# A long convolution whose weight rows hold two lags 1024 apart, and a ring of its own for VectorE's linear terms

## The chip, the cores and the metric

The kernel runs on one core of one Trainium2 chip. The metric is the device time of one execution in microseconds (us). The time before is the median of three executions, 815.14 us (814.76 to 815.46). The profile was taken in one further execution, with a time of its own, 807.64 us.

## The reference

Two independent blocks share one output of 2048 x 1024 in bf16; each fills 512 of its columns.

```python
# A: attention, S = 2048, D = 512, 32 heads of 16
qkv = x @ wqkv                              # (2048, 1536)
p = softmax(q @ k.T * 16 ** -0.5)           # per head, 2048 x 2048
a = concat_heads(p @ v) @ wo
# B: gated long convolution, per channel c of 512
k_shift[t] = sum_j k[t - j] * shift_k[c, j]          # 4 taps
kv = k_shift * v
y[t] = sum_{l <= t} ssm_k[c, l] * kv[t - l] + ssm_D[c] * kv[t]   # through an FFT of 4096
b = q * y
out = concat(a, b)
```

## The kernel before, in words

**Attention.** Work is cut into 2048 blocks of 128 keys x 512 queries of one head, 64 blocks for each of 32 groups (`NQB * NG`). A counter `T` counts chunks. For each chunk TensorE (the score matmuls of `qk_mm`, line 796) writes two or three blocks of scores into banks of PSUM, and ScalarE takes the exponential of all of them in one instruction (`emit_exp`, line 821) and writes bf16 into a ring of `R_PT` slots, `PT`. Two sets of three banks alternate, so that ScalarE works on one while TensorE fills the other. Two chunks later `pv_step` and `emit_pv` (line 970) multiply `PT` with V and add into bank `PVB`; at the end of a group VectorE transposes the sums (line 1041), divides and transposes back.

**Exponentials on VectorE.** In some chunks one more block (`dve_block`, `exp_on_dve`) goes to bank `BGB` or to the third bank, and VectorE computes its exponential. Line 884 moves the scores out as bits (`lin`). Then two such blocks, a pair of 128 x 1024, take five operations: `mant` (892), `power` (896), `line` (899), `square` (902) and `cube` (905). A block done so enters the product with V as three terms, `lin`, `low` and `top`, so as three matmuls instead of one. The three terms of a pair lie in the ring `PTD` of `R_PTD` = 3 pairs; the mantissa lies in one buffer, `FR`, so `mant` of a pair waits for `square` of the pair before (`h_last`).

**Convolution.** 64 steps (`qd`) take eight channels each. The reversed convolution kernel lies in a scratch in DRAM; each row of the ring `WR` (`R_W` = 12 rows of 2048, four rows for a step) is one DMA of 512 KB from it: 64 copies, each shifted by one element more, of the kernels of two channels, on alternate partitions. `conv_lags` (line 1187) multiplies `WR` with `KV`. `KV` holds kv of two channels side by side with zeros between, so half of each weight tile is zero. A step has 32 lags (`NLAG`), and a lag is four matmuls of 128 columns, one for each strip of 32 columns of the array. After a burst of two steps `conv_out` (line 1207) copies the sums to `YB`; after four steps `conv_turn` (line 1219) transposes them, VectorE multiplies with q (line 1226), and they go out through `QN`. `kv` itself comes from units `("kv", c, i)`: line 512 applies the four taps with matmuls of 128 columns, line 561 multiplies with v in two halves, and `spread_kv` lays it out in `KV` with four DMAs for each quarter of the channels.

**What sets the order.** A planner in Python writes out the order of every engine beforehand. It keeps an assumed time of its own for each engine and each DMA, and it puts projections, convolution, VectorE blocks and fillers where they fit in front of the next exponential: `emit_qk`, `late_block`, `pv_step`, `emit_bg` (units and convolution, with due times from `jobs`, `conv_due` and `PLAN`), `release` (loads of `WR`) and `warm_up` (fillers without use, line 1382) for each `T`. Loads of `WR` are issued by SyncE (SP), the loads of q and the results by GpSimd (POOL). On the chip each engine runs its list in that order and waits on semaphores.

Of the kernel before, what the change touches and what calls it, by code (L numbers as in the profile page):

```python
# [13 lines left out]
S = 2048  # L14
# [13 lines left out]
NLAG = S // 64  # L28
# [4 lines left out]
R_W = 12  # L33
R_PT = 16
# [8 lines left out]
LEAD = 2  # L43
YIELD = -4
FIRST = 6
BURST = 2
OVER_C = 0.0
HURRY = 2
LOW = 4.5
# [20 lines left out]
R_PTD = 3  # L70
# [12 lines left out]
PLAN = 588  # L83
# [4 lines left out]
GAP = 5  # L88
# [7 lines left out]
DMA_KB = 394  # L96
X_KB = 200
# [157 lines left out]
def bass_concat_heads__mha_block__ssm_conv_h3__prompt_kernel(  # L255
# [24 lines left out]
    def sb(name, shape, dt=BF16):  # L280
# [9 lines left out]
    WR = sb("WR", [128, R_W, S])  # L290
# [3 lines left out]
    QN = QNF[:, 0:NB * 256].rearrange("p (t d) -> p t d", t=NB)  # L294
# [13 lines left out]
    PTD = sb("PTD", [128, R_PTD, 3, 2, QB])  # L308
    FR = sb("FR", [128, 2 * QB])
# [7 lines left out]
           for x in (WR[:, R_W - 2, :], WR[:, R_W - 1, :], OUTA[:, :, :].rearrange("p r d -> p (r d)"), VS2[:, :])]  # L317
# [9 lines left out]
    KVF = KV[:, :, :, :, :].rearrange("p o r u g -> p (o r u g)")  # L327
    STG = [KVF[:, 32 * S // 16 * ((c + 1) % 4):32 * S // 16 * ((c + 1) % 4 + 1)].rearrange(
        "p (h o u k g) -> p h o u k g", h=2, o=16, u=NB, k=2) for c in range(4)]
    XN = FR[:, :].rearrange("p (j f) -> p j f", j=2)  # L330
# [66 lines left out]
    d_wr = [DmaSem(sem(f"d_wr{i}")) for i in range(3)]  # L397
# [25 lines left out]
    for c in range(4):  # L423
        src = bass.AP(tensor=v2.tensor, offset=v2[128 * (NB - 1), 128 * c].offset, ap=[[D, 128], [-128 * D, NB], [1, 128]])
        h_vn.append(dma(sp, d_kv[3 + c], VST[c], src, kb=512))
# [18 lines left out]
    h_kv0 = [None, None]  # L444
    h_kv0[0] = pool.op(lambda e: e.memset(KV[:, :, :, :, :].rearrange("p o r u g -> p (o r u g)").bitcast(U32), 0), us=(8.8, 8.9))
# [25 lines left out]
    def ready(u):  # L471
# [8 lines left out]
        return KT_OF[u[1]][0] in h_kt and (u[1] < 3 or h_kv0[1] is not None and at(h_kv0[1]) <= pe.t)  # L480

    def pe_unit(u, bank, parts=(0, 1, 2, 3)):
# [19 lines left out]
        elif kind == "kv":  # L502
# [5 lines left out]
            def mm(e, b):  # L508
                ins = None
                for m in range(4):  # L510
                    c0 = LEFT + 128 * (4 * i + 3 - b) - m
                    ins = e.matmul(PS[:, bank, 128 * b:128 * b + 128], lhsT=KTR[kt_i][:, kt_c, c0:c0 + 128], rhs=DG[:, c, m, :],  # L512
                                   start=(m == 0), stop=(m == 3))
                return ins
# [19 lines left out]
    def evac_unit(u, bank, h):  # L534
# [18 lines left out]
        elif kind == "kv":  # L553
            _, c, i = u
            u0 = NB - 4 - 4 * i
            val = VST[c][:, u0:u0 + 4, :].rearrange("p b (h o g) -> p b h o g", h=2, g=4)
            src = PS[:, bank, :].rearrange("p (b h o g) -> p b h o g", b=4, h=2, g=4)
            for ch in range(2):
                dst = STG[c][:, ch, :, u0:u0 + 4, ch, :].rearrange("p o u g -> p u o g")
                hh = (dve.op if ch else urgent)(  # L560
                    lambda e, dst=dst, ch=ch: e.tensor_tensor(dst, src[:, :, ch], val[:, :, ch], ALU.mult),
                    [h, h_vn[c], h_kv0[c // 3]], us=(0.335, 0.46))
# [3 lines left out]
            if sum(kv_n[0:2]) == 8 and c < 2:  # L566
                load_qn(0, [h])
                open_wr(2, hh, True)
# [13 lines left out]
    def spread_kv(c, hh):  # L582
        for half in range(2):
            for ch in range(2):
                src = STG[c][64 * half:64 * half + 64, ch].rearrange("p o u k g -> p o (u k g)")
                dst = KV[ch:128:2, 16 * c:16 * c + 16, 1 - half, :, :].rearrange("p o u g -> p o (u g)")
                h_kvc[c] = dma(sp, d_kvc[c], dst, src, [hh, h_kvc[c - 1] if c else None] if half + ch == 0 else [], kb=256, rate=210)
# [20 lines left out]
    def kz_store(us):  # L608
# [4 lines left out]
        open_wr(R_W - 2, h_kzw[0])  # L613
# [111 lines left out]
    def emit_qk(T):  # L725
# [12 lines left out]
        bl = next_blocks(n + (extra in next_blocks(n)))  # L738
        if extra in bl:
            bl.remove(extra)  # L740
# [30 lines left out]
    def next_blocks(n):  # L771
        bl = []
        for b in [b for b in queue[:LOOK] if blk_group(b) == blk_group(queue[0])] + queue[:n]:
            if len(bl) < n and b not in bl and (blk(b)[2] not in [blk(x)[2] for x in bl] or len(bl) + 1 > 4):
                bl.append(b)
        for b in queue[:n]:
            if len(bl) < n and b not in bl:
                bl.append(b)
        return bl
# [55 lines left out]
    def conv_due():  # L835
        return N_OPEN + state["qd"] * (PLAN - N_OPEN) / (C // 8)

    def conv_wants(T):
        qd = state["qd"]
        return (state["started"] and T >= conv_due() - YIELD and qd < C // 8 and wr_next[0] >= qd + BURST and h_kvc[qd // 16] is not None  # L840
                and at(h_wr[qd + BURST - 1], h_kvc[qd // 16]) + WAIT < pe.t + 1.0 and not (state["turn"] and qd % 4 == 4 - BURST))

# [3 lines left out]
    def dve_block(T, n_act, aside=True):  # L846
        if T < T_DVE or aside and busy() or len(queue) < LAST_BLKS + 3 * TAIL_GAP + 4:
            return None
        if aside and conv_wants(T):
            return None  # L850
# [8 lines left out]
        bl = next_blocks(n_act + 1)  # L859
        x = sub(bl[-1])  # L860
        left = len([b for b in queue if sub(b) == x])
        if left - 3 >= 2.6 * GAP:
            return bl[-1]
# [6 lines left out]
        rows = [blk(b)[2] for b in bl[:-1]]  # L870
        ahead = [b for b in ahead[:4] if b not in bl]
# [646 lines left out]
```

## Time and profile before

| What | Before |
|---|---|
| median of three executions | 815.14 us |
| profiled execution, its own time | 807.64 us |
| its span, first to last instruction | 805.7 us |
| ScalarE (ACT) busy | 784.9 us |
| VectorE (DVE) busy | 715.1 us |
| TensorE (PE) busy, matmul | 745.7 us |
| mean share of the 16 DMA engines, queue of SP | 58.2% |
| mean granted TensorE clock | 0.999 |

In rows of groups, the numbers after the bar are the busy time of the group in us (the time that its instructions cover together), the mean time of one in ns, and the time that the engine sat idle just before them, with what ended it. An instruction can start before the one ahead of it on its engine has ended, so its mean time is longer than the distance from one start to the next.

### The profile page before, as it was taken

What the parts mean: (1) busy time and instruction counts of PE and PEld (TensorE: products, weight loads), DVE (VectorE), ACT (ScalarE), POOL (GpSimd) and SP (SyncE); (2) the same over time, 40 slices, a digit from 0 to 9 for tenths busy, and PEclk for the clock granted to TensorE, in tenths of its full rate; (3) what the DMA queues carried; (4) which work ended last, traced back from release to release, by engine and by line L of the source; (5) the groups of instructions that cost most, each with busy time, mean ns of one, the idle gap of its engine ahead of it and who ended that gap; (6) DMA issues with size and microseconds to landing.
All of it is one profiled execution on the core that took longest, in us unless ns stands there. A gap on an engine that the chain in (4) does not pass through costs nothing.

```text
span 805.7 us, 31982 instructions
## 1 busy us (share of the span) xinstructions
PE 745.7 (93%) x14505; PEld 337.1 (42%) x14505; DVE 715.1 (89%) x1427; ACT 784.9 (97%) x680; POOL 90.4 (11%) x160
## 2 busy tenths in 40 slices
PE   8889998999998989999999989989989899999987
PEld 3333444435444433444433434434443434434444
DVE  5989999999798989898898989889999899889986
ACT  7999999999999999999999999999999999999997
POOL 6200402020100101020010030101003020000000
PEclk9999999999999999999999999999999999999999
DMA  9995277846877671446845657985684663876310
GB/s 244 204 306 175 63 184 227 287 108 215 265 261 240 215 243 59 156 115 235 267 142 206 213 168 254 308 281 193 227 299 138 212 224 129 283 260 216 110 55 28
DMA packets 88101, 161.44 MB, mean 200 GB/s; under 512 B 49216, under 2 KB 53184, under 8 KB 87584
## 3 DMA queue, kind: packets, MB, share of 16 engines
q1 hardware_dynamic: 80976, 150.43, 58.2%
q0 software_dynamic: 5792, 8.66, 3.7%
q8 instruction: 114, 1.87, 0.9%
q10 hardware_dynamic: 1200, 0.33, 0.2%
q14 instruction: 19, 0.16, 0.1%
HBM read 142.87 MB, written 6.42 MB: 185 GB/s over the span
## 4 chain that ended last, share of the span: by engine, by line
ACT 79%; PE 14%; DVE 5%; issue 1%; DMA 1%
ACT PT L821 79%; PE PS L970 5%; PE PS L796 4%; PE PS L1187 1%; DVE PTD L884 1%; DMA QN<-in_B_k_dram 1%; PE PS L512 1%; PE PS L1115 1%; PE PS L630 0%; PE PS L491 0%; DVE PTD L902 0%; DVE DT L1041 0%; DVE PTD L905 0%; DVE FR L892 0%; DVE PTD L896 0%
## 5 line engine op out<-in xcount | busy, mean ns | idle before, releaser
L821 ACT ACTIVATE PT<-PS 128x1024 bf16<-128x1024 f32 (+1 forms) x674 | 781.9, 1362 | 11.5 <-PE PS L796 10.8
L796 PE MATMUL PS<-QT,KTo 32*128 32x512 bf16 (+2 forms) x2248 | 265.6, 364 | 39.8 <-ACT PT L821 17.5
L884 DVE TENSOR_SCALAR PTD<-PS 128x512 uint16<-128x512 f32 x326 | 219.2, 682 | 49.2 <-PE PS L796 47.8
L1187 PE MATMUL PS<-WR,KV 128*26 128x128 bf16 (+9 forms) x8192 | 191.2, 219 | 0.7 <-issue 0.6
L970 PE MATMUL PS<-PT,VA 128*32 128x512 bf16 (+2 forms) x1889 | 184.6, 369 | 5.0 <-DVE DT L1041 2.1
L1187 PEld LDWEIGHTS PS<-WR,KV 128*32 128x32 bf16 (+8 forms) x8192 | 140.6, 94 | 52.9 <-issue 29.8
L796 PEld LDWEIGHTS PS<-QT,KTo 32*128 32x128 bf16 x2248 | 69.6, 91 | 205.0 <-ACT PT L821 150.4
L970 PE MATMUL PS<-PTD,VA 128*32 128x512 bf16 (+1 forms) x1077 | 121.0, 360 | 3.9 <-issue 3.9
L902 DVE TENSOR_TENSOR PTD<-FR,PTD 128x1024 f16<-128x1024 bf16 (+1 forms) x164 | 112.3, 685 | 4.0
L905 DVE TENSOR_TENSOR PTD<-PTD 128x1024 bf16<-128x1024 f16 (+1 forms) x164 | 111.5, 680 | 1.9
L352 POOL DMA_DIRECT2D QT<-QS x120 | 60.4, 511 | 443.7 <-DVE QS L539 443.7
L970 PEld LDWEIGHTS PS<-PT,VA 128*32 128x32 bf16 x1889 | 47.4, 93 | 100.8 <-issue 85.5
L892 DVE TENSOR_SCALAR FR<-PTD 128x1024 uint16<-128x1024 uint16 (+1 forms) x164 | 69.0, 421 | 3.5
L896 DVE TENSOR_SCALAR PTD<-PTD 128x1024 uint16<-128x1024 uint16 (+1 forms) x164 | 68.9, 420 | 0.0
L1382 PE MATMUL PS<-IDN,ZW 128*32 128x512 bf16 (+3 forms) x297 | 67.4, 310 | 1.3 <-issue 1.0
L899 DVE TENSOR_SCALAR PTD<-FR 128x1024 f16<-128x1024 bf16 (+1 forms) x164 | 68.1, 415 | 0.0
L970 PEld LDWEIGHTS PS<-PTD,VA 128*32 128x32 bf16 x1077 | 44.8, 96 | 33.2 <-issue 4.4
L1382 PEld LDWEIGHTS PS<-IDN,ZW 128*32 128x32 bf16 x297 | 23.4, 96 | 23.3 <-issue 12.2
L1041 DVE STREAM_TRANSPOSE DT<-PS 128x512 f32<-128x512 f32 x31 | 22.1, 713 | 5.6 <-PE PS L970 5.3
L352 POOL DMA_DIRECT2D out_dram<-OUTA x15 | 8.6, 575 | 97.2 <-DVE OUTA L1123 93.1
L1115 PE MATMUL PS<-WKV,OTN 128*128 128x512 bf16 (+1 forms) x68 | 19.0, 371 | 0.3 <-DVE OTN L1090 0.3
L523 PE MATMUL PS<-WKV,xT 128*128 128x128 bf16 x256 | 18.3, 220 | 0.4 <-DVE KTo L548 0.3
(75 smaller groups left out, 259.3 us busy)
## 6 DMA issues: line engine op xcount, KB each, us to landing
WR<-kz_scratch SPq DMA_DIRECT2D x256, 512.0 KB, 5.8
KV<-KV SPq DMA_DIRECT2D x16, 256.0 KB, 5.4
kz_scratch<-WR SPq DMA_DIRECT2D x1, 2176.0 KB, 8.8
QN<-in_B_q_dram POOLq DMA_DIRECT2D x2, 1024.0 KB, 7.6
out_dram<-QN POOLq DMA_DIRECT2D x2, 1024.0 KB, 8.3
QT<-QS POOLq DMA_DIRECT2D x120, 16.0 KB, 3.3
out_dram<-OUTA POOLq DMA_DIRECT2D x15, 128.0 KB, 2.0
QN<-in_B_ssm_k_dram SPq DMA_DIRECT2D x1, 1024.0 KB, 8.3
```

What stands on the lines that cost most here:

```text
L352: f(outp, inp).then_inc(dsem.sem, 16)
L796: ins = e.matmul(PS[:, bank, i * w:i * w + w], lhsT=KTo[32 * s:32 * s + 32, OF[n_] % 2, kt * 128:(kt + 1) * 128], rhs=QT[32 * s:32 * s + 3 ...
L821: h_exp[T] = act.op(lambda e: e.activation(PT[:, p0:p0 + n, :].rearrange("p b f -> p (b f)"), PS[:, banks[0]:banks[0] + n, :].rearrange("p ...
L884: st["h"].append(urgent(lambda e: e.tensor_scalar(lin[:, QB * half:QB * half + QB].bitcast(U16), PS[:, bank, :], FIX_ADD, FIX_HI, ALU.add, ...
L892: st["d"] = st["m"] = dve.op(lambda e: e.tensor_scalar(FR[:, w].bitcast(U16), lin[:, w].bitcast(U16), 0x7F, 0x3F80, ALU.bitwise_and, ALU.b ...
L896: dve.op(lambda e: e.tensor_scalar(low[:, w].bitcast(U16), lin[:, w].bitcast(U16), 0xFF80, None, ALU.bitwise_and), [st["h"][-1]], us=us)
L899: st["d"] = dve.op(lambda e: e.tensor_scalar(top[:, w].bitcast(FP16), FR[:, w], T1, T0, ALU.mult, ALU.add), [st["m"]], us=us)
L902: st["d"] = h_last[j] = dve.op(lambda e: e.tensor_tensor(top[:, w].bitcast(FP16), FR[:, w], top[:, w].bitcast(FP16), ALU.mult), [st["d"]], ...
L905: st["d"] = dve.op(lambda e: e.tensor_tensor(top[:, w], top[:, w].bitcast(FP16), lin[:, w], ALU.mult), [st["d"]], us=us)
L970: ins = e.matmul(dst, lhsT=w, rhs=rhs, start=first, stop=last, tile_position=(0, 32 * s))
L1187: ins = e.matmul(PS[32 * g:32 * g + 2 * ((30 - d) // 2 + 1), BGB, c0:c0 + w], lhsT=kv, rhs=WR[:, (4 * qd + g) % R_W, S - 64 * d - 128:S - ...
L1382: pe.op(lambda e, s=s, k=k, rhs=rhs, bank=bank, rows=rows, c0=c0, first=first: e.matmul(PS[32 * s:32 * s + rows, bank, c0:c0 + 128 * k], l ...
```

## The change

- `KV` holds kv of one channel group with no second channel and no zeros between: partitions 0 to 63 hold one half, and partitions 64 to 127 the positions 1024 away. A row of `WR` is 1024 wide: its first 64 partitions start at lag 0, the last 64 at lag 1024. `R_W` is 24 rows of 256 KB, so the ring has its old size.
- A step now takes four channels, so there are 128 (`NQD`). It has eight lags (`NLAG` = 8); a lag is again four matmuls with 128 columns to stream, whose results go to two runs of 64 columns. A burst is four steps. The steps alternate between two quarters of the channels (`kv_of`), so the convolution starts when two quarters of kv are there.
- `spread_kv` is one DMA for a quarter instead of four, and line 561 is one operation of 512 instead of two of 256; the taps are matmuls with weight tiles of 64 columns, twice as many. `YB` is copied 512 at a time, and `conv_turn` uses matmuls with a permuted identity, two instead of one transpose. The clearing of a part of `KV` in mid-run is gone. The loads of q and the stores of b through `QN` are cut in two halves of 64 partitions.
- VectorE's pairs: `lin` has a ring of its own, `PTD` of five pairs; `low` and `top` lie in `RST` of three pairs (`R_RST`); `FR` is gone: the mantissa lies where `low` will be, and the order is now mant, line, square, power, cube. `PT` has 14 slots instead of 16.
- The planner chooses the rows of blocks so that they differ (`next_blocks`, `pick_row`), and some of its numbers change.

```diff
-NLAG = S // 64
+NLAG = S // 256
+NQD = C // 4
-R_W = 12
-R_PT = 16
+R_W = 24
+R_PT = 14
-FIRST = 6
-BURST = 2
+FIRST = 4
+BURST = 4
-LOW = 4.5
+LOW = 3.5
-R_PTD = 3
+R_PTD = 5
+R_RST = 3
-PLAN = 588
+PLAN = 600
-GAP = 5
+GAP = 7
...
-    KV = sb("KV", [128, C // 8, 2, 2 * NB, 4])
+    KV = sb("KV", [128, NQD, 2 * NB, 4])
-    PTD = sb("PTD", [128, R_PTD, 3, 2, QB])
-    FR = sb("FR", [128, 2 * QB])
+    PTD = sb("PTD", [128, R_PTD, 2, QB])
+    RST = sb("RST", [128, R_RST, 2, 2, QB])
...
-                    ins = e.matmul(PS[:, bank, 128 * b:128 * b + 128], lhsT=KTR[kt_i][:, kt_c, c0:c0 + 128], rhs=DG[:, c, m, :],
-                                   start=(m == 0), stop=(m == 3))
+                    for x in range(2):
+                        c0 = LEFT + 64 * (4 * i + 3 - b) + S // 2 * x - m
+                        ins = e.matmul(PS[64 * x:64 * x + 64, bank, 128 * b:128 * b + 128], lhsT=KTR[kt_i][:, kt_c, c0:c0 + 64],
+                                       rhs=DG[:, c, m, :], start=(m == 0), stop=(m == 3), tile_position=(0, 64 * x))
...
+        src = KV[0:64, 32 * c:32 * c + 32, 0:NB, :].rearrange("p q w g -> p q (w g)")
+        dst = KV[64:128, 32 * c:32 * c + 32, NB:2 * NB, :].rearrange("p q w g -> p q (w g)")
+        h_kvc[c] = dma(sp, d_kvc[c], dst, src, [hh, h_kv0, h_kvc[c - 1] if c else None], kb=256, rate=KV_KB)
...
-            row = 128 * (qd // 16) + 4 * (qd % 16) + g
-            src = bass.AP(tensor=kz_ap.tensor, offset=kz_ap[row, 0].offset, ap=[[1, 64], [64 * LKZ, 2], [1, S]])
-            h_wr[qd] = dma(sp, d_wr[qd % 3], WR[:, n % R_W, :], src, [h_kzw[0], dep, h], kb=512, rate=WR_KB, late=2.95)
+            src = bass.AP(tensor=kz_ap.tensor, offset=kz_ap[channel(qd) + g, 0].offset, ap=[[S // 2, 2], [1, 64], [1, S // 2]])
+            h_wr[qd] = dma(sp, d_wr[qd % (R_W // 4)], WR[:, n % R_W, :], src, [h_kzw[0], dep, h], kb=256, rate=WR_KB, late=2.95)
...
             for n in range(n0, n1):
-                d = DIST[n]
-                w = 64 if d < 0 else 128
                 for g in range(4):
-                    kv = KV[:, qd, (1 + d) % 2, (1 + d) // 2 * 2:2 * NB, g]
-                    ins = e.matmul(PS[32 * g:32 * g + 2 * ((30 - d) // 2 + 1), BGB, c0:c0 + w],
-                                   lhsT=kv, rhs=WR[:, (4 * qd + g) % R_W, S - 64 * d - 128:S - 64 * d - 128 + w],
+                    dst = PS[32 * g:32 * g + 32 - 2 * n, BGB, :]
+                    c0 = 256 * (1 - pair) + 64 * (1 - half)
+                    dst = bass.AP(tensor=dst.tensor, offset=PS[32 * g:32 * g + 1, BGB, c0:c0 + 1].offset, ap=[dst.ap[0], [128, 2], [1, 64]])
+                    w0 = S // 2 - 128 * n - 128
+                    ins = e.matmul(dst, lhsT=KV[:, channel(qd) // 4, 2 * n:2 * NB, g], rhs=WR[:, (4 * qd + g) % R_W, w0:w0 + 128],
                                    start=(n == 0), stop=(n == NLAG - 1), tile_position=(0, 32 * g))
...
-                ins = e.transpose(pbf[:, 128 * k:128 * k + 128], YB[:, b % 2, 128 * k:128 * k + 128], IDN[:, :])
+                for part in range(2):
+                    y = YB[:, k // 2, 256 * (k % 2) + 128 * part:256 * (k % 2) + 128 * part + 128]
+                    ins = e.matmul(PS[:, bank, 128 * k + 4 * part:128 * k + 128], lhsT=y, rhs=(own, next_)[part], start=part == 0, stop=part == 1)
...
-        begin = lambda: (n == 2 or st["alone"]) and (j == 0 or j - 1 in h_last)
+        begin = lambda: (n == 2 or st["alone"]) and (j < R_RST or all((j - R_RST, i) in h_ptd for i in range(len(pairs[j - R_RST]["h"]))))
...
-        if aside and conv_wants(T):
+        if aside and conv_wants(T) and (state["go"] or conv_due() < T - PRESS):
```

More of the change, by code (lines that the diff above doesn't have):

```diff
@@ L858, in dve_block, with pick_row @@
             return None
[L859 to L860 removed]
+        def pick_row(of, most):
+            mine = [b for b in of if sub(b) == sub(of[0])][:most]
+            there = [blk(b)[2] for b in on_dve if sub(b) == sub(of[0]) and on_dve[b] not in h_ptd]
+            return min(mine, key=lambda b: there.count(blk(b)[2]))
+        x = sub(queue[min(n_act, len(queue) - 1)])
         left = len([b for b in queue if sub(b) == x])
+        if left - 3 >= 2.6 * GAP and sub(queue[0]) == x:
+            return pick_row(queue, LOOK)
         if left - 3 >= 2.6 * GAP:
[L863 removed]
+            return pick_row(queue[n_act:], 4)
         if x == subs[-1]:
@@ L869, in dve_block @@
             return None
-        rows = [blk(b)[2] for b in bl[:-1]]
-        ahead = [b for b in ahead[:4] if b not in bl]
-        return next((b for b in ahead if blk(b)[2] not in rows), ahead[0] if ahead else None)
+        return pick_row(ahead, 4)
     h_last = {}
@@ L949, in emit_pv @@
             pv_n[(n, s)] = pv_n.get((n, s), 0) + 1
-            terms = [PTD[:, on_dve[b][0] % R_PTD, i, on_dve[b][1], :] for i in range(3)] if b in on_dve else [PT[:, pt_of[b], :]]
+            terms = [PT[:, pt_of[b], :]] if b not in on_dve else [PTD[:, on_dve[b][0] % R_PTD, on_dve[b][1], :]] + [
+                RST[:, on_dve[b][0] % R_RST, i, on_dve[b][1], :] for i in range(2)]
             hl = 2 * s + n % 2
@@ L991, in conv_done @@
     def conv_done():
-        return state["qd"] == C // 8 and not state["turn"] and not part[0]
+        return state["qd"] == NQD and not state["turn"] and not part[0]
     def pv_step(T):
```

159 lines of the change are left out of this document (79 added, 80 removed).

## The prediction

> **What bounds the kernel now.** I read the page first, its parts 1, 4 and 5, then the groups of ScalarE with the shapes kept apart, then who waits for whom.
>
> ```profile
> span 805.7 us, 31982 instructions
> PE 745.7 (93%) x14505; PEld 337.1 (42%) x14505; DVE 715.1 (89%) x1427; ACT 784.9 (97%) x680; POOL 90.4 (11%) x160
> ...
> ACT 79%; PE 14%; DVE 5%; issue 1%; DMA 1%
> ...
> L821 ACT ACTIVATE PT<-PS 128x1024 bf16<-128x1024 f32 (+1 forms) x674 | 781.9, 1362 | 11.5 <-PE PS L796 10.8
> L884 DVE TENSOR_SCALAR PTD<-PS 128x512 uint16<-128x512 f32 x326 | 219.2, 682 | 49.2 <-PE PS L796 47.8
> L1187 PE MATMUL PS<-WR,KV 128*26 128x128 bf16 (+9 forms) x8192 | 191.2, 219 | 0.7 <-issue 0.6
> L970 PE MATMUL PS<-PTD,VA 128*32 128x512 bf16 (+1 forms) x1077 | 121.0, 360 | 3.9 <-issue 3.9
> L1382 PE MATMUL PS<-IDN,ZW 128*32 128x512 bf16 (+3 forms) x297 | 67.4, 310 | 1.3 <-issue 1.0
> ```
>
> ScalarE carries 79% of the chain that ended last. Its exponentials cover 781.9 of 805.7 us, and in the whole run they waited only 11.5 us, nearly all of it for TensorE's scores. So the span is the exponentials (781.9), their waits (11.5) and about 12 us at the two ends. TensorE looks as busy, but 67.4 us of it are fillers (line 1382), and VectorE is idle for 805.7 − 715.1 = 90.6 us, of which 49.2 lie before line 884: it waits for a block to work on.
>
> ```profile
> L821 ACT ACTIVATE PT<-PS 128x1536 bf16<-128x1536 f32 x374 | 524.9, 1558 | 2.8 <-PE PS L796 2.5
> L821 ACT ACTIVATE PT<-PS 128x1024 bf16<-128x1024 f32 x300 | 301.1, 1117 | 8.7 <-PE PS L796 8.3
> ```
>
> ScalarE does 374 x 3 + 300 x 2 = 1722 of the 2048 blocks, VectorE 326. The waits sit on the short exponentials: 8.7 us over 300 (29 ns each) against 2.8 over 374 (7.5 ns).
>
> **ScalarE, which sets the end.** The written order of the changed program has 438 exponentials of three blocks, 191 of two and one of one: 1697 blocks in 630 instructions. VectorE takes 351 blocks, 25 more. I need the distance from one exponential to the next.
>
> ```profile
> 31.16 12.19 ACT L821 ACTIVATE PT<-PS 128x1536 bf16<-128x1536 f32 x9
> 789.36 6.73 ACT L821 ACTIVATE PT<-PS 128x1024 bf16<-128x1024 f32 x7
> 796.35 1.02 ACT L821 ACTIVATE PT<-PS 128x1024 bf16<-128x1024 f32 x1 [0.25 <-PE PS L796]
> 797.83 2.88 ACT L821 ACTIVATE PT<-PS 128x1024 bf16<-128x1024 f32 x3 [0.46 <-PE PS L796]
> ```
>
> In the timeline (start, length, then the merged instructions) nine of three blocks take 12.19 us: (12.19 − 1.56) / 8 = 1.329. For two blocks the rows give (2.88 − 1.117) / 2 = 0.88 and (6.73 − 1.117) / 6 = 0.936; spreading 781.9 − 374 x 1.329 over 300 gives 0.95, small stalls included. I take 0.915, the middle. A single one is about 0.915 − 0.441 = 0.47, with 0.441 the difference of the two means. The sum: 64 x 1.329 − 109 x 0.915 + 0.47 = 85.1 − 99.7 + 0.5 = −14.1 us. With 0.88 it is −10.4, with 0.95 −18.0. Both ends of the run stay as they are.
>
> The waits of 11.5 us: by the new mix, 191 x 29 ns + 438 x 7.5 ns = 8.8, a gain of 2.7. Against it stands a fuller VectorE, below, whose price no row gives. I set the two against each other and keep 11.5; the bounds are 0 and, in the rival, well above.
>
> **TensorE, beside it.**
>
> ```profile
> 399.87 0.63 PE L1187 MATMUL PS<-WR,KV 128*14 128x128 bf16 x32
> ...
> 400.79 0.51 PE L1187 MATMUL PS<-WR,KV 128*6 128x128 bf16 x24
> ...
> L512 PE MATMUL PS<-OTN,QN 128*128 128x128 bf16 x128 | 9.4, 220 | 1.6 <-DMA QN<-in_B_k_dram 1.0 <-DVE KV L561 0.3 <-DVE PTD L884 0.3
> L1219 PE MATMUL PS<-IDN,YB 128*128 128x128 bf16 x64 | 6.4, 222 | 1.4 <-DVE YB L1207 1.4
> ```
>
> Eight convolution matmuls more take 0.63 − 0.51 = 0.12 us, so a lag of four takes 0.06. The 2048 lags become 1024: −61 us. The taps are 512 matmuls instead of 256; between nothing (two tiles of 64 columns run together) and 256 x 9.4 / 128 = 18.8 us (they do not). I take nothing: the page shows tiles of 32 columns together, the 1077 matmuls of line 970 covering 121.0 us where their mean is 360 ns. The turn is 128 instead of 64: +6.4. The 25 blocks on VectorE add two matmuls each, 50 x 121.0 / 1077 = +5.6. So −30 to −49 us, of which fillers take much back (481 instead of 297 in the written order). None of it is on the path by itself: ScalarE waited 11.5 us for TensorE. What it buys is room in front of the exponentials, in which VectorE gets its further blocks; that is counted already.
>
> What no row shows is a matmul that writes two runs of 64. I price it as one run of 128, the nearest row, and keep twice 0.06 as the other end; a gain below 0.06 is excluded, since the same 128 columns stream.
>
> **VectorE, close behind.**
>
> ```profile
> 401.35 0.42 DVE L1207 CAST YB<-PS 128x256 bf16<-128x256 f32 x1 [0.18 <-PE PS L1187]
> 401.69 0.68 DVE L902 TENSOR_TENSOR PTD<-FR,PTD 128x1024 f16<-128x1024 bf16 x1
> 402.49 0.69 DVE L1226 TENSOR_TENSOR QN<-PS,QN 128x512 bf16<-128x512 bf16 x1
> 403.10 0.68 DVE L905 TENSOR_TENSOR PTD<-PTD 128x1024 bf16<-128x1024 f16 x1
> 403.70 0.42 DVE L892 TENSOR_SCALAR FR<-PTD 128x1024 uint16<-128x1024 uint16 x1
> 404.04 0.42 DVE L896 TENSOR_SCALAR PTD<-PTD 128x1024 uint16<-128x1024 uint16 x1
> 404.37 0.42 DVE L899 TENSOR_SCALAR PTD<-FR 128x1024 f16<-128x1024 bf16 x1
> 404.82 0.69 DVE L902 TENSOR_TENSOR PTD<-FR,PTD 128x1024 f16<-128x1024 bf16 x1
> 405.55 0.69 DVE L905 TENSOR_TENSOR PTD<-PTD 128x1024 bf16<-128x1024 f16 x1
> ```
>
> Start to start: 0.34 for mant, power and line, 0.60 for a tensor_tensor of 1024 and, by the multiplication at 402.49 (0.61), for a read of 512 from PSUM. An operation that needs the result of the one right ahead starts later: square 0.45 after line instead of 0.34, cube 0.73 after square instead of 0.60, so about 0.12 each. Added: 25 evictions x 0.60 = 15.0; twelve pairs more (174 for 162) x (3 x 0.34 + 2 x 0.60 = 2.22) = 26.6; one more half pair, at most half of that, 1.1; `YB` 32 x (0.60 − 0.34) = 8.3; kv 16 x 0.61 − 32 x 0.34 = −1.1. Together +50. Taken away: by the written order 290 operations before follow directly on the one that they need (118 squares, 56 cubes, 61 mants on the square that frees `FR`, 55 mants on an eviction); after it are 177 (56 squares, 59 lines, 30 powers, 32 mants), since two pairs can now interleave. 113 x 0.12 = −13.6. Net +36 us.
>
> ```profile
> 0.00:40.00 40.00, 35.41 (x316) 14.09 (x317) 30.15 (x62) 34.66 (x31) 17.78 (x24) 1.00 0.96 224
> ...
> 120.00:760.00 640.00, 596.97 (x12325) 269.66 (x12320) 575.35 (x1136) 632.03 (x548) 59.85 (x112) 1.00 0.64 213
> 760.00:806.00 46.00, 38.82 (x903) 21.40 (x901) 36.21 (x83) 40.38 (x37) 2.81 (x4) 0.98 0.12 37
> ```
>
> In these stretches (length, then PE, weight loads, DVE, ACT and POOL busy, then granted clock, DMA share, GB/s) VectorE is idle for 9.9 us in the first and 9.8 in the last. Of its 90.6 idle us 71 lie between. After, 791.6 − (715.1 + 36) = 40.5, so 21 between: 3% of it. So VectorE stays behind ScalarE by the sum, with little left.
>
> **Transfers.**
>
> ```profile
> WR<-kz_scratch SPq DMA_DIRECT2D x256, 512.0 KB, 5.8
> KV<-KV SPq DMA_DIRECT2D x16, 256.0 KB, 5.4
> ...
> FR<-in_A_x_dram SPq DMA_DIRECT2D x1, 256.0 KB, 3.3
> ...
> SPq L352 <- PE PS L796: 412.1, 89, 31.0
> ...
> POOL KV L1194 <- PE PS L1187: 46.0, 1, 46.0
> ```
>
> The ring loads carry the same 134 MB in 512 DMAs of 256 KB with rows of 2 KB, where rows were 4 KB. A load of 256 KB with rows of 1 KB landed in 3.3 us, one of 512 KB with rows of 4 KB in 5.8: shorter rows show no doubled price. The middle stretch uses 0.64 of the DMA engines; I count nothing. [...]
>
> SP issues 256 more DMAs; it waits 412.1 us for scores to time them, so they hide there, and twelve fewer for `KV`. Behind a late ring load on SP stand only the next ones and, at the end, the last store. On POOL the wait of 46.0 us for clearing `KV` goes; behind it stood loads of q, which are due 20 chunks ahead: nothing. Convolution starts when two quarters of kv are there instead of one, so later by a few units of line 512; ScalarE has its blocks meanwhile: nothing, unless it pushes convolution into the end of the run.
>
> **The forecast.** 807.64 − 14.1 = 793.5 for a profiled execution. The median of the runs lies 7.5 above the profiled one; I keep that: 815.14 − 14.1 = 801.0 us. What a measurement of this kernel can tell from no change is about 0.2%, 1.6 us.
>
> **Rivals.** First: VectorE becomes a second bound, but only in part. For: 21 us of slack in some 750, when before it had 71. Against: the 49.2 us of waiting were for blocks that TensorE had not brought. If a third to all of the 21 us has to be idle again and ScalarE waits for it, the end moves by 7 to 21 us, less where waits coincide: I put 5 to 12, so 806 to 813.
>
> Second, on the slower side: group ends. At each of 31 of them the last product with V needs the last pair's cube, and TensorE's list stops there; the next scores stand behind it, and ScalarE runs dry. Before, VectorE's slack kept this off. If one square and one cube, 0.60 + 0.73, are still to do at each end, it is 31 x 1.33 = 41 us, less the 14.1: 842. It decides for slower from 14.1 / 31 = 0.45 us at each end. For: the fuller VectorE. Against: blocks for VectorE may now be chosen only further from a group's end (`GAP` 7 for 5).
>
> Third: the two-run matmul takes 0.12 a lag. Then 61 us of TensorE come where the order left no room; the fillers' gaps take some, half of it moves the scores: +30 − 14.1, so 831. For: no row shows the form; against: nothing else in it changes. A late ring (each row behind its step) would show in the same place, at line 1198.
>
> Fourth: the change yields more, as the short exponentials' waits go with the room on TensorE: half of 11.5 gone and 0.936 for the short ones (64 x 1.329 − 109 x 0.936 + 0.47 = −16.5): −22, so 793.
>
> **Numbers.** Forecast 0.56 (797 to 805), fourth 0.12, first 0.18, second and third together 0.14. Faster: the first three of these, less 0.02 for a first rival that goes on to no change: 0.84; same 0.03 and slower 0.13. The range from 793 to 812 leaves out the slower ones and little at the low end: about 0.18.
>
> **What would show it.** Right: line 821 x630 with about 768 us busy and some 11 us of waits; convolution x4096; VectorE near 751 busy and its wait before the eviction (line 888) far below 49.2. Wrong: waits of line 821 above 20 us, named by scores that themselves waited for `RST` or `PTD` (first and second), or by line 1198 with a lag above 0.06 (third).

## The result: 2794.38 us, 3.43 times the time before

Four executions of the changed kernel gave a median of 2794.38 us (2793.9 to 2795.27), beside 814.95 us for the kernel before, with one execution more than in the table above; the ratio is 3.434 (3.420 to 3.447). The forecast was 801.0 us with a range from 793 to 812.

From parts 1 to 5 of the page of the changed kernel:

```profile
span 2792.8 us, 25210 instructions
PE 902.6 (32%) x10969; PEld 344.5 (12%) x10969; DVE 761.2 (27%) x1501; ACT 794.9 (28%) x636; POOL 90.7 (3%) x163
...
PEclk9955555576555656555775565655655657555568
...
q1 hardware_dynamic: 102352, 147.27, 14.5%
...
SPq 51%; DMA 32%; PE 9%; DVE 4%; ACT 3%; issue 1%
...
L821 ACT ACTIVATE PT<-PS 128x1536 bf16<-128x1536 f32 (+2 forms) x630 | 791.9, 1339 | 1988.5 <-PE PS L796 1986.1
...
L1198 PE MATMUL PS<-WR,KV 128*18 128x128 bf16 (+7 forms) x4096 | 155.9, 297 | 1829.7 <-DMA WR<-kz_scratch 1787.3
```

The work is close to what the prediction said: 630 exponentials, 4096 convolution matmuls, exponentials that cover 791.9 us (about 768 were forecast; e9 below has 769.1). All the rest is waiting. ScalarE waited 1986.1 us for scores (line 796), and ahead of the convolution (line 1198) TensorE waited 1787.3 us for ring loads; the scores stand behind those matmuls in TensorE's list. Before, 79% of the chain that ended last was ScalarE's; now SP's queue and the DMAs have 83%. Yet the SP queue's transfers took only 14.5% of 16 engines' time, for nearly the bytes of before. That share of 16 is as much as 2.3 engines always busy: the DMA engines are far from full. The low clock (0.623 over the run) comes with a TensorE that is busy for 32% of the span.

The timeline of the changed kernel over 40 us (start, length, merged instructions, idle time before them and its releaser):

```profile
199.06 61.78 SPq L353 DMA_DIRECT2D WR<-kz_scratch  x12
...
212.62 1.05 PE L1198 MATMUL PS<-WR,KV 128*32 128x128 bf16 x32 [17.82 <-DMA WR<-kz_scratch]
...
214.27 1.45 ACT L821 ACTIVATE PT<-PS 128x1536 bf16<-128x1536 f32 x1 [18.40 <-PE PS L796]
233.12 1.05 PE L1198 MATMUL PS<-WR,KV 128*32 128x128 bf16 x32 [18.90 <-DMA WR<-kz_scratch]
...
235.20 1.87 PE L1227 MATMUL PS<-IDN,YB 128*128 128x128 bf16 x8
```

and SP's queue of the kernel before:

```profile
50.46 6.67 SPq L352 DMA_DIRECT2D WR<-kz_scratch  x10
```

SP needs 61.78 / 12 = 5.15 us for each 256 KB load, where before it needed 0.67 us for one of 512 KB. A step of the convolution takes four loads: 4 x 5.15 = 20.6 us, and the two steps in the timeline start 233.12 − 212.62 = 20.5 us apart. By the trace the convolution's first matmul starts at 167.0 us and its last at 2741.2: 2574 of the 2792.8 us, 20.3 for each step. The last line of the timeline holds a second, small surprise: eight of the turn's matmuls last 1.87 us, more than 32 of the convolution.

In the other kernels below the lines are shifted by up to 12: scores are at 796 to 807, exponentials at 821 to 832, the eviction at 888 to 899, convolution at 1198 to 1210, the turn at 1227 to 1239.

### The profile page after: what moved, and what is told of

The parts are those of the page before. It is cut to its first block, busy times and chain, and to the rows that moved or that the text cites. A ratio compares the mean times of both kernels' runs of the same rounds, so it can differ in the third digit from the quotient of the medians.

```text
span 2792.8 us, 25210 instructions
## 1 busy us (share of the span) xinstructions
PE 902.6 (32%) x10969; PEld 344.5 (12%) x10969; DVE 761.2 (27%) x1501; ACT 794.9 (28%) x636; POOL 90.7 (3%) x163
## 3 DMA queue, kind: packets, MB, share of 16 engines
q1 hardware_dynamic: 102352, 147.27, 14.5%
## 4 chain that ended last, share of the span: by engine, by line
SPq 51%; DMA 32%; PE 9%; DVE 4%; ACT 3%; issue 1%
SPq L353 51%; DMA WR<-kz_scratch 32%; ACT PT L821 3%; PE PS L975 3%; PE PS L796 2%; PE PS L1198 2%; DVE PTD L888 1%; DMA KV<-KV 1%; DVE RST L909 1%; PE PS L1395 0%; DVE RST L903 0%; PE PS L1227 0%; DVE RST L896 0%; DVE RST L900 0%; DVE RST L906 0%
## 5 line engine op out<-in xcount | busy, mean ns | idle before, releaser
L821 ACT ACTIVATE PT<-PS 128x1536 bf16<-128x1536 f32 (+2 forms) x630 | 791.9, 1339 | 1988.5 <-PE PS L796 1986.1
L1198 PE MATMUL PS<-WR,KV 128*18 128x128 bf16 (+7 forms) x4096 | 155.9, 297 | 1829.7 <-DMA WR<-kz_scratch 1787.3
L1198 PEld LDWEIGHTS PS<-WR,KV 128*18 128x18 bf16 (+7 forms) x4096 | 99.0, 126 | 1896.3 <-DMA WR<-kz_scratch 1653.8
L1395 PE MATMUL PS<-IDN,ZW 128*32 128x512 bf16 (+3 forms) x481 | 125.1, 357 | 0.0
L903 DVE TENSOR_TENSOR RST<-RST 128x1024 f16<-128x1024 bf16 (+1 forms) x177 | 119.4, 677 | 1.8
L909 DVE TENSOR_TENSOR RST<-RST,PTD 128x1024 bf16<-128x1024 f16 (+1 forms) x177 | 119.2, 674 | 0.0
L975 PE MATMUL PS<-RST,VA 128*32 128x512 bf16 (+1 forms) x774 | 119.1, 427 | 0.0
L896 DVE TENSOR_SCALAR RST<-PTD 128x1024 uint16<-128x1024 uint16 (+1 forms) x177 | 74.2, 422 | 67.7 <-PE PS L975 66.7
L900 DVE TENSOR_SCALAR RST<-RST 128x1024 f16<-128x1024 bf16 (+1 forms) x177 | 73.5, 418 | 1.9
L906 DVE TENSOR_SCALAR RST<-PTD 128x1024 uint16<-128x1024 uint16 (+1 forms) x177 | 73.1, 414 | 0.9
L975 PEld LDWEIGHTS PS<-RST,VA 128*32 128x32 bf16 x774 | 42.7, 111 | 38.6 <-issue 21.0
L1046 DVE STREAM_TRANSPOSE DT<-PS 128x512 f32<-128x512 f32 x31 | 22.1, 711 | 11.2 <-PE PS L975 10.7
```

Of the source, the lines that this page charges most:

```text
L821: h_exp[T] = act.op(lambda e: e.activation(PT[:, p0:p0 + n, :].rearrange("p b f -> p (b f)"), PS[:, banks[0]:banks[0] + n, :].rearrange("p ...
L896: st["d"] = dve.op(lambda e: e.tensor_scalar(low[:, w].bitcast(U16), lin[:, w].bitcast(U16), 0x7F, 0x3F80, ALU.bitwise_and, ALU.bitwise_or ...
L900: st["d"] = dve.op(lambda e: e.tensor_scalar(top[:, w].bitcast(FP16), low[:, w], T1, T0, ALU.mult, ALU.add), [st["d"]], us=us)
L903: st["d"] = dve.op(lambda e: e.tensor_tensor(top[:, w].bitcast(FP16), low[:, w], top[:, w].bitcast(FP16), ALU.mult), [st["d"]], us=us)
L906: dve.op(lambda e: e.tensor_scalar(low[:, w].bitcast(U16), lin[:, w].bitcast(U16), 0xFF80, None, ALU.bitwise_and), [st["d"]], us=us)
L909: st["d"] = dve.op(lambda e: e.tensor_tensor(top[:, w], top[:, w].bitcast(FP16), lin[:, w], ALU.mult), [st["d"]], us=us)
```

## The experiments

My theory after the result: a load is carried by as many DMA engines as the outermost dimension of its access pattern allows. The load of before was `[[1, 64], [64 * LKZ, 2], [1, S]]`, 64 outermost; the changed one is `[[S // 2, 2], [1, 64], [1, S // 2]]`, 2 outermost. The rivals were the shorter rows (2 KB for 4 KB), the number of loads (512 for 256), and addresses 1024 elements apart. Where an expectation speaks of the ledger, it means the sums of the prediction.

**e1_paired: 64 outermost again.** One load brings two ring rows for one half of the partitions.

```diff
-            src = bass.AP(..., offset=kz_ap[channel(qd) + g, 0].offset, ap=[[S // 2, 2], [1, 64], [1, S // 2]])
-            ... WR[:, n % R_W, :], src, ...
+            x, r = g % 2, n % R_W - g % 2
+            src = bass.AP(..., offset=kz_ap[channel(qd) + g - x, S // 2 * x].offset, ap=[[1, 64], [LKZ, 2], [1, S // 2]])
+            ... WR[64 * x:64 * x + 64, r:r + 2, :], src, ...
```

> Same program as the changed kernel, same number and size of ring loads (512 of 256 KB, rows of 2 KB); only the order of dimensions in a load differs: one load brings the first halves of two ring rows (64 partitions outermost), the next their second halves. Theory A (a load is spread over as many DMA engines as its outermost dimension allows, and 2 allows two): the loads go back to about 0.6 us of issue, the convolution no longer waits, and the time is that of the ledger, 793 to 812 us. Theory B (small loads or rows of 2 KB cost 5 us each whatever their shape): about 2790 us. Theory C (the new convolution matmuls or the low clock are the cause): about 2790 us.

**e2_outer4 and e3_outer8: 4 and 8 outermost,** with the same bytes, rows and number of loads.

```diff
-ap=[[S // 2, 2], [1, 64], [1, S // 2]]
+ap=[[256, 4], [1, 32], [1, S // 2]]      # e2
+ap=[[128, 8], [1, 16], [1, S // 2]]      # e3
```

> The changed kernel with one edit: the source of a ring load has an outermost dimension of 4 (4 times 32 rows) instead of 2; same count, rows and bytes, other lags land in the partitions, so the convolution multiplies other data. Theory A: a load takes 2.5 us instead of 5.04, 512 of them 1290 us, and with the 213 us that the changed kernel spends beside its loads 1400 to 1600 us. Theories B and C: about 2790 us.

> As with an outermost dimension of 4, but 8 (8 times 16 rows); the convolution again multiplies other data. Theory A: 1.26 us a load, 645 us in all, less than the exponentials take, but the planner counts 0.78 us a load, so bursts come late now and then: 800 to 950 us. Theories B and C: about 2790 us.

**e4_before_outer2: the kernel before, with 2 outermost.**

```diff
-ap=[[1, 64], [64 * LKZ, 2], [1, S]]
+ap=[[64 * LKZ, 2], [1, 64], [1, S]]
```

> The kernel before with one edit: the two dimensions of a ring load's source are swapped, 2 outermost instead of 64; 256 loads of 512 KB with rows of 4 KB as before, landing in other partitions, so the convolution multiplies other data. Theory A: 64 rows of 4 KB for each of two engines at about twice the price of 2 KB, 10 us a load, 256 loads 2600 us, with some 200 beside them 2600 to 2900 us. Theory B: 815 us, since count and rows are those of before. Theory C: 815 us.

Measured: e1 879.0 us (873.29 to 886.12), ratio 1.079 (1.073 to 1.085); and in single executions e2 1489.2 us, e3 913.7 us, e4 2711.79 us. The last three lie where theory A expected them; e1 is far from B and C, but 67 us above A's range. SP's queue in the timeline of e2, 4 outermost, and its DMA queue on the page (packets, MB, share of 16 engines):

```profile
299.67 41.52 SPq L353 DMA_DIRECT2D WR<-kz_scratch  x16
...
q1 hardware_dynamic: 103376, 147.28, 27.5%
```

The same of e3, 8 outermost:

```profile
304.88 36.29 SPq L353 DMA_DIRECT2D WR<-kz_scratch  x26
...
q1 hardware_dynamic: 105424, 147.28, 46.4%
```

The timeline of e4, the kernel before with 2 outermost:

```profile
596.79 103.55 SPq L352 DMA_DIRECT2D WR<-kz_scratch  x11
```

The same of e1, 64 outermost:

```profile
50.53 9.74 SPq L353 DMA_DIRECT2D WR<-kz_scratch  x14
```

A 256 KB load takes SP 5.15 us with 2 outermost, 2.6 with 4, 1.4 with 8 and 0.70 with 64. Times the outermost dimension the first three are nearly one value: 2 x 5.15 = 10.3, 4 x 2.6 = 10.4, 8 x 1.4 = 11.2. No view names the engine that carries a row; three more readings bear on their number. For the same 512 loads the queue has 102352 packets in the changed kernel, 1024 more in e2 (2 a load), 3072 more in e3 (6 a load) and 7168 more in e1 (14 a load, its line is below): one packet for each further engine, if they are 2, 4, 8 and 16. In the kept traces the ring rows under way at the same time are most often 2 in the changed kernel (for 2377 us) and, while there are any, 16 in the kernel before, with 64 outermost (for 192 us). On the pages the mean share of the 16 DMA engines stands in most of the 40 slices at 1 tenth in the changed kernel and in e4 (0.13 in the former from 180 to 260 us; 2 of 16 are 0.125), at 2 in e2 (4 of 16 are 0.25) and at 5 in e3 (8 of 16 are 0.5). e4 also shows that neither the shorter rows nor the number of loads is needed: the kernel before, with its own 256 loads of 4 KB rows, goes from about 815 to 2712 us by this one edit, at 103.55 / 11 = 9.4 us a load. The addresses 1024 apart are out too, since e4 has none. So the readings agree with 2, 4, 8 and 16 engines for 2, 4, 8 and 64 outermost, as theory A has it for the first three; what sets 16 for 64 is not shown.

So e1 is 2794 − 879 = 1915 us faster than the changed kernel. But it is still 7.9% slower than before, where the ledger gave a gain. Two things could be seen in its page (queue; exponentials; convolution and turn; ring loads, with the median time from issue to landing last):

```profile
q1 hardware_dynamic: 109520, 147.30, 73.3%
...
L821 ACT ACTIVATE PT<-PS 128x1536 bf16<-128x1536 f32 (+2 forms) x630 | 777.5, 1362 | 81.7 <-PE PS L796 79.8
...
L1199 PE MATMUL PS<-WR,KV 128*18 128x128 bf16 (+7 forms) x4096 | 95.0, 225 | 19.1 <-issue 15.8
...
L1228 PE MATMUL PS<-IDN,YB 128*128 128x128 bf16 (+1 forms) x128 | 30.1, 388 | 1.8 <-DVE YB L1215 0.9
...
WR<-kz_scratch SPq DMA_DIRECT2D x512, 256.0 KB, 7.9
```

First, the queue's transfers took 73.3% of 871.6 us = 639 us of 16 engines, where before it was 58.2% of 805.7 = 469 us. Second, the 128 matmuls of the turn cover 30.1 us, not the 12.8 of the ledger (6.4 + 6.4). The turn is a part of the change; loads that fill one half of the partitions came in with e1 alone, as the changed kernel's fill all 128. Each was tried by itself.

**e5_full_width: a load again fills all 128 partitions.** Like the change itself, with the two outer dimensions swapped.

```diff
-ap=[[S // 2, 2], [1, 64], [1, S // 2]]
+ap=[[1, 64], [S // 2, 2], [1, S // 2]]
```

> The changed kernel with the first two dimensions of a ring load's source swapped, 64 outermost: one load fills all 128 partitions of one ring row, as before; the lags land in other partitions, so the convolution multiplies other data. Against the run with loads of 64 partitions, which took 879 us with 512 loads of the same size and an unchanged written order. Theory P (a load that fills 64 partitions moves at about half the rate of one that fills 128: a row of 2 KB took 144 ns there and 84 ns when two engines had it alone; late ring rows and late code then hold TensorE up): packets back near 84 ns, about 50 us less, 815 to 840 us. Rival Q (512 loads instead of 256 delay TensorE's code whatever their rate): 860 to 880 us.

**e6_paired_perm and e7_full_width_perm: the turn reads its permuted identity from a tile of its own,** `PERM`, written once at the start, instead of columns of `IDN` 32 apart in falling order; e6 is e1 with it, e7 is e5 with it. Two small tables move into `YB` to make room for it.

```diff
-        own, next_ = [bass.AP(..., offset=IDN[0:1, 31:32].offset, ap=[IDN[:, :].ap[0], [-1, n], [32, 4]]) for n in (32, 31)]
+        own, next_ = PERM[:, 0:128], PERM[:, 0:124]
```

> The run with loads of 64 partitions, and one more edit: the permuted identity of the turn is copied once into a tile of its own, so that its matmuls read 128 adjacent columns instead of columns 32 apart. Eight of them took 1.87 us there, where eight of adjacent columns take some 0.5. Theory S (the stepped read costs the time): the turn falls to about 0.5 us, and with 16 turns of 1.4 us less the time falls by 10 to 23 us, to 856 to 869 us. Rival R (what costs is that two matmuls add into one place, or fp32 results): the turn stays at 1.87 us and the time at 879 us.

> Both edits: loads of 128 partitions with 64 outermost (the convolution multiplies other data) and the permuted identity in a tile of its own. Theories P and S together: nothing is left between the written order and the ledger, 793 to 812 us. If VectorE is a second bound, 806 to 830 us with waits of TensorE for VectorE; if P fails, about 860 us.

| Ring load | turn from `IDN` | turn from `PERM` |
|---|---|---|
| one half of the partitions, two rows each | e1 879.0, ratio 1.079 (1.073 to 1.085) | e6 859.09, ratio 1.053 (1.049 to 1.058) |
| all partitions, one row each | e5 820.18, ratio 1.007 (1.004 to 1.010) | e7 796.72, ratio 0.978 (0.975 to 0.982) |

Both terms are real, and they nearly add: the load is worth 59 to 62 us, the turn 20 to 23. The change's own two faults are therefore the order of the dimensions, 2794.38 − 820.18 = 1974 us by e5, which differs from the changed kernel in that order alone, and the turn. The turn's group in e6:

```profile
L1231 PE MATMUL PS<-PERM,YB 128*128 128x128 bf16 (+1 forms) x128 | 11.4, 239 | 2.5 <-issue 1.2 <-DVE YB L1218 0.9
```

The page of e5:

```profile
q1 hardware_dynamic: 109520, 147.30, 58.4%
...
L821 ACT ACTIVATE PT<-PS 128x1536 bf16<-128x1536 f32 (+2 forms) x630 | 772.9, 1379 | 28.7 <-PE PS L796 27.2
...
WR<-kz_scratch SPq DMA_DIRECT2D x512, 256.0 KB, 4.9
```

58.4% of 813.9 us is 475 us of engines, for the same packets and bytes as e1's 639, and a load lands in 4.9 us instead of 7.9. ScalarE waits 28.7 us instead of 81.7.

A further run, e8, was to write a new order for e6's slower loads; it gave no result, so whether another order would suit them is not known.

**e9_full: the whole change with the loads and the turn repaired.** Ring rows lie as in e7; kv is laid out to fit them, one half of the positions on even and the other on odd partitions, by three DMAs for each quarter instead of one. The orders of TensorE and ScalarE are those of the changed kernel.

```diff
+    def stage(c):
+        return KV[:, 32 * c + 32:32 * c + 64, 0:NB, :] if c < 3 else OUTA[...]
...
-        src = KV[0:64, 32 * c:32 * c + 32, 0:NB, :].rearrange(...)
-        dst = KV[64:128, 32 * c:32 * c + 32, NB:2 * NB, :].rearrange(...)
+        part = [(0, 0, 0), (1, 1, 0), (1, 0, NB)]
+        src = [stage(c)[64 * half:64 * half + 64, :, :, :].rearrange(...) for x, half, w0 in part]
+        dst = [KV[x:128:2, 32 * c:32 * c + 32, w0:w0 + NB, :].rearrange(...) for x, half, w0 in part]
```

> The changed kernel with the full computation and both causes taken away: ring loads of 128 partitions with 64 outermost, kv laid out to match (the two halves on alternate partitions, three transfers for each quarter instead of one, from a staging place), and the permuted identity in a tile of its own. TensorE's and ScalarE's written orders are those of the changed kernel. If nothing but the two causes stood between the ledger and the result: 793 to 800 us, about 18 us under the kernel before. If the layout of kv with runs of 128 bytes costs time at the start of the convolution: 800 to 810 us.

Measured: 797.11 us (796.43 to 798.36), ratio 0.980 (0.977 to 0.983). This is the change as it was meant, and it beats both kernels. Its page:

```profile
span 795.3 us, 25183 instructions
PE 706.3 (89%) x10933; PEld 293.7 (37%) x10969; DVE 750.3 (94%) x1501; ACT 772.1 (97%) x636; POOL 91.4 (11%) x164
...
q1 hardware_dynamic: 126032, 149.40, 61.1%
...
ACT 65%; DVE 19%; PE 14%; issue 1%
...
L831 ACT ACTIVATE PT<-PS 128x1536 bf16<-128x1536 f32 (+2 forms) x630 | 769.1, 1394 | 13.8 <-PE PS L806 13.2
...
L1405 PE MATMUL PS<-IDN,ZW 128*32 128x512 bf16 (+3 forms) x481 | 112.1, 326 | 0.0
L1208 PE MATMUL PS<-WR,KV 128*18 128x128 bf16 (+7 forms) x4096 | 90.7, 221 | 1.2 <-issue 1.2
...
L898 DVE TENSOR_SCALAR PTD<-PS 128x512 uint16<-128x512 f32 x351 | 239.2, 684 | 3.7 <-PE PS L806 2.5
```

and its groups of TensorE:

```profile
L1237 PE MATMUL PS<-PERM,YB 128*128 128x128 bf16 (+1 forms) x128 | 9.8, 220 | 1.5 <-DVE YB L1224 0.9
L521 PE MATMUL PS<-OTN,QN 128*64 128x128 bf16 x256 | 9.4, 221 | 0.8 <-DVE PTD L898 0.8
L521 PE MATMUL PS<-OTN 128*64 128x128 bf16 x256 | 8.9, 221 | 0.4 <-DVE PTD L898 0.4
```

**e10_conv_alone: e9 with VectorE's pairs as before** (`PTD` of three pairs with three terms, `FR`, `PT` of 16 slots). Its written order has 451 exponentials of three blocks, 189 of two and one of one, and 316 blocks on VectorE.

```diff
-    PTD = sb("PTD", [128, R_PTD, 2, QB])
-    RST = sb("RST", [128, R_RST, 2, 2, QB])
+    PTD = sb("PTD", [128, R_PTD, 3, 2, QB])
+    FR = sb("FR", [128, 2 * QB])
```

> That kernel with VectorE's part undone: PTD of three pairs for all three terms, FR for the mantissa, 16 slots in PT, the old order of the five operations; the planner writes a new order, which has 451 exponentials of three blocks, 189 of two and one of one, 1732 blocks on ScalarE, 10 more than before. By the ledger (77 x 1.329 - 111 x 0.915 + 0.5) +1 us on the kernel before, 811 to 820 us: the convolution without zeros alone gives nothing, since one buffer for the mantissa keeps VectorE from taking more blocks. Rival: the room on TensorE alone brings the gain, since fewer scores come late: 797 to 808 us.

Measured: 803.81 us (803.09 to 803.98), ratio 0.988 (0.983 to 0.992). The page of e10:

```profile
L830 ACT ACTIVATE PT<-PS 128x1536 bf16<-128x1536 f32 (+1 forms) x641 | 782.0, 1475 | 7.4 <-PE PS L805 6.9
...
L896 DVE TENSOR_SCALAR PTD<-PS 128x512 uint16<-128x512 f32 x316 | 213.9, 684 | 46.1 <-PE PS L805 45.2
```

The exponentials cover what they did before, 782.0 against 781.9 us, as VectorE takes ten blocks fewer. They wait 7.4 us instead of 11.5. The expected 811 to 820 us were missed, and the rival's 797 to 808 came. So the convolution's part, with its own written order, is worth something without a block moved to VectorE, about 1.2%, and VectorE's part the other 0.8%: 803.81 − 797.11 = 6.7 us. VectorE's part without the convolution's was not run.

**e11_halves: the change with each load cut into two,** each one row for 64 partitions, 1024 loads of 128 KB.

```diff
+            src = [bass.AP(..., offset=kz_ap[channel(qd) + g, S // 2 * x].offset, ap=[[1, 64], [1, S // 2]]) for x in range(2)]
+            dst = [WR[64 * x:64 * x + 64, n % R_W, :] for x in range(2)]
```

> The changed kernel with each ring load cut in two loads of 64 partitions of one row (1024 loads of 128 KB); the turn as in the changed kernel. It tells what halved the rate in the first run of the study, where a load filled 64 partitions with two rows each. If the 64 partitions do: the same share of the DMA engines for the same bytes (639 us of 16 engines there), 870 to 930 us. If two rows for a partition do: some 475 us of 16 engines as with full width, 815 to 845 us.

Measured: 914.79 us in one execution. Its page:

```profile
q1 hardware_dynamic: 117712, 147.33, 53.9%
...
WR<-kz_scratch SPq DMA_DIRECT2D x1024, 128.0 KB, 3.1
```

53.9% of 913.1 us is 492 us of engines: here loads that write one half of the partitions do not cost e1's price. But SP starts one only every 0.64 us (1024 x 0.64 = 655 us), and the rows are late by the number of loads: two of 0.64 us make 1.28 us a row, near the 1.4 of e3, whose 913.7 us the time is near to as well. The time lies in the range of the one theory and the share of the engines at the value of the other, so e11 tells neither. 128 KB in 0.64 us are also no more than 205 GB/s. e12 and e13 were made to tell it.

**e12_alternate: e9 with e1's loads on every other partition** instead of one half of them. **e13_two_rows: e9 with one load of 512 KB for two rows of all 128 partitions.**

```diff
+            x, r = g % 2, n % R_W - g % 2                                   # e12
+            ... ap=[[1, 64], [LKZ, 2], [1, S // 2]] -> WR[x:128:2, r:r + 2, :]
+            ... ap=[[1, 128], [LKZ, 2], [1, S // 2]] -> WR[:, r:r + 2, :]   # e13, for even g
```

> The complete computation of e9_full with one thing changed: a load fills 64 partitions with two ring rows each, as in e1_paired, but every other partition (the even ones, then the odd ones) instead of one half of the partitions. What made e1's loads take 639 us of 16 engines where e5's took 475 is tested, with three theories. Half: loads that write only partitions 0 to 63, or only 64 to 127, go at about half rate. Two rows: a partition that gets two rows in one load is what costs. Count: 64 partitions cost, wherever they lie. Half expects e9's time, 797 us (794 to 801), and about 61% of the span on that queue. Two rows and Count expect the time of e6_paired_perm, 859 us (850 to 865), and about 74% on the queue. [...] Against Half speaks e11_halves, whose loads also write one half of the partitions and took 492 us of 16 engines.

> As e9_full, but one load of 512 KB fills 128 partitions with two ring rows each, where e9 has two loads of one row each; a partition's rows are other lags, so the convolution multiplies other data. Half and Count expect e9's time or a little more, since the second row comes with the first and both land later: 795 to 812 us, and about 58 to 62% of the span on that queue. Two rows expects 850 to 870 us and about 74% on the queue.

Measured: e12 798.67 us (797.26 to 799.78), ratio 0.977 (0.975 to 0.979); e13 799.4 us (796.85 to 803.82), ratio 0.980 (0.975 to 0.984). The queue and the ring loads on the page of e12:

```profile
q1 hardware_dynamic: 126032, 149.40, 58.7%
...
WR<-kz_scratch SPq DMA_DIRECT2D x512, 256.0 KB, 4.8
```

The same of e13:

```profile
q1 hardware_dynamic: 121936, 149.38, 59.8%
...
WR<-kz_scratch SPq DMA_DIRECT2D x256, 512.0 KB, 6.7
```

Neither 64 partitions as a number (e12: 58.7% of 795.8 = 467 us of engines) nor two rows for a partition (e12 again, and e13: 59.8% of 795.7 = 476 us) is what cost e1 its 639 us. Between e1's layout and e12's only the place of the 64 partitions differs: one half, or every other one. Why that place matters is not shown. The page's rows of DMA share (tenths in 40 slices) and GB/s in e1

```profile
DMA  9995159999918699799956889999993875994110
GB/s 263 218 232 111 28 103 230 236 224 236 233 31 194 152 233 206 152 231 230 255 128 148 179 185 232 234 246 286 270 241 91 226 181 141 220 234 128 27 25 27
```

and in e12

```profile
DMA  9896065999606387787916668889861845863200
GB/s 254 192 286 197 8 115 180 336 265 364 223 8 213 121 290 237 204 271 245 325 70 178 181 227 281 275 275 329 303 236 36 283 156 170 275 234 114 55 2 29
```

show that e1's engines move less while they are as busy: beyond the sixth slice, those at 9 (90% or more) move some 233 GB/s in the median in e1 (18 slices) and 329 in e12 (5). e11 has no such slice there; its loads come at 205 GB/s at most, below those 233, which may be why. It was not tried.

## Why the prediction was wrong, point by point

**Transfers: the step that failed.** It reads "shorter rows show no doubled price ... I count nothing". The loads were sized by bytes and by row length, from rows for other loads, and the shape of the access pattern, which the quoted diff shows, was not looked at. Shorter rows were indeed nearly free: e5, which has them, took 475 us of 16 engines where the 4 KB rows of the kernel before took 469. What cost 1974 us (e5) of the 1993 by which the forecast missed is 2 instead of 64 outermost, by the readings above 2 instead of 16 DMA engines for a load.

**"SP issues 256 more DMAs; ... so they hide there."** With 64 outermost this holds: e9's 512 loads lie on SP at 0.7 us each, and it is faster than before. With 2 outermost the instruction on SP lasts 5.15 us, about as long as the transfer by an estimate (64 rows for each of two engines at 84 ns, the median of a row in the changed kernel's trace, are 5.4 us), and the 412.1 us in which SP waited for scores were no cover for 512 x 5.15 = 2637 us.

**The third rival named the place and not the price.** "A late ring would show in the same place, at line 1198": that is where the 1787.3 us stand. Its own mechanism, a dearer matmul into two runs of 64, did not occur: 221 ns in the mean (e9) against 219, and 4096 cover 90.7 us where 8192 covered 191.2.

**The turn, a mis-sized term.** Forecast +6.4 us for 64 matmuls more, by a row of matmuls with a packed right-hand side. Measured: 30.1 us covered (e1) where the ledger has 12.8, and 20 to 23 us of run time. The operand, columns of the identity 32 apart in falling order, was not priced. From `PERM` the 128 matmuls cover 9.8 us (e9). Two matmuls that add into one place, the rival in e6, are still there, so they are not the cause; whether the distance or the falling order is was not separated.

**TensorE otherwise.** The taps cost nothing, as taken: 9.4 + 8.9 = 18.3 us for 512, below the 18.8 that 256 come to by the rate quoted. The saving was put too low, at −30 to −49 us: without the fillers TensorE was busy for about 745.7 − 67.4 = 678 us before and is for 706.3 − 112.1 = 594 us in e9, −84. The lag was priced at 0.06 us by the step from 24 to 32 matmuls; by the groups it is 191.2 / 2048 = 0.093. And "none of it is on the path by itself" was too strong: e10 gains 1.2% with no block moved to VectorE, 4.1 us of it less waiting in the profiled executions. Those two differ by 3.5 us only (spans of 805.7 and 802.2); the rest of the 9.8 us between the medians is that the kernel before mostly ran slower than in its profiled execution.

**ScalarE and VectorE: right, once nothing else is in the way.** In e9 ScalarE's exponentials cover 769.1 us (forecast about 768) and wait 13.8 (11.5); VectorE is busy for 750.3 us (751), its wait before the eviction is 3.7 us instead of 49.2. Forecast for a span without the 1.9 us around it: 805.7 − 14.1 = 791.6; measured 795.3, and 2.3 of the 3.7 us between are those waits. The first and second rival, VectorE as a bound and dry group ends, did not come: the chain gives VectorE 19%, but ScalarE's waits rise by 2.3 us only. The 7.5 us kept between profiled execution and median were not there in e9 (797.02 and 797.11), so 797.1 comes out below the 801.0 of the forecast; that it comes so near is in part luck, as a span 3.7 us too short and an offset of 7.5 us too many went against each other. The record hints at where the offset comes from, without an experiment on it: over all runs of this study the kernel before had 12 executions with a granted clock of 0.998 or more, with a median of 813.0 us, and 7 below 0.991, with 819.7, while e9 always had 0.997 or more. The 0.2% that the prediction takes for noise is too small by the same executions, which lie between 809.56 and 822.75 us.

## What to carry to other kernels

When a diff reorders the dimensions of a DMA's access pattern, read its outermost dimension first, then which partitions it writes, before its bytes: 2 instead of 64 outermost made this kernel 3.4 times slower with the same bytes in rows of the same length (2794.38 against 820.18 us), and writing two rows to one half of the partitions instead of every other one cost 60 us more (e6 859.09, e12 798.67). When the DMA queue's share on the page falls while matmuls wait for DMAs (here from 58.2% to 14.5%), ask how many engines carry the transfers before blaming the memory. A sum over engines can be right term by term and the forecast still wrong, so each operand's and each transfer's pattern wants a row of the trace with that very pattern, or a wide bound.

## What was not expected of the hardware

- The time of the issuing instruction on SP falls as the outermost dimension grows: 5.15, 2.6 and 1.4 us for 256 KB with 2, 4 and 8 (the changed kernel, e2, e3), and 0.70 with 64 (e1); 9.4 us for 512 KB in 4 KB rows with 2 (e4). If two engines carry a load with 2 outermost, one moves 256 KB / (2 x 5.15 us) = 25 GB/s, as an estimate.
- A 256 KB load with 64 outermost, two rows to each of 64 partitions, lands in 7.9 us (median, e1) when these are one half of the partitions and in 4.8 us (e12) when they are every other one.
- Eight matmuls of 128 columns take 1.87 us (e1, and the changed kernel), 0.23 each, when the streamed operand takes four columns 32 apart, then the four one column lower, and so on; with a packed operand 128 of them cover 9.8 us (e9), 0.08 each.
- In e1 convolution matmuls stood still for 15.8 us in seven places for which the trace shows no releaser; in e9, with the queue at 61.1% instead of 73.3%, for 1.2 us. That late code held them, as the expectation of e5 supposes, is not shown.
